# Shared transposes, one state load per batch and turned state reads in a fused attention kernel on one core

## The chip, the core and the metric

The program runs on one core of a Trainium2 chip: TensorE (PE; its weight loads are shown as PEld), VectorE (DVE), ScalarE (ACT), GpSimd (POOL) and SyncE (SP), which here issues every DMA. The metric is the time of one launch in device microseconds, the median of several runs.

## The reference

Inputs are x (8 batches, 8 heads, 512 positions, 64 wide), state (8, 8, 32, 64), a gate, and query, key and value weights for 4 experts, with an output weight for each. Per batch and head:

```
a     = softmax(x state^T / 8);   xread = a state      # x reads the state
a2    = softmax(state x^T / 8);   sread = a2 x         # the state reads x
X     = [xread; sread], heads side by side             # 544 rows of 512
w     = softmax over the best 2 of the 4 gate logits X w_gate
q,k,v = X wq[e], X wk[e], X wv[e]                       # 64 wide
y     = sum over e of w_e * causal_softmax(q k^T / 8) v wo[e]
```

## The kernel before

Most operands are kept as an fp16 high part and an fp16 remainder, so that a product is three matmuls (PROD). A batch has 512 rows, four tiles of 128 positions, and 32 state rows, which two batches share in a tail.

For each batch `front` (`first` for batch 0) splits x into parts and transposes them (xT<-xh), scores x against the state and back (`state_scores`), and makes gs, v, keys (kt) and queries. Queries leave PSUM through `masked` (qf), are split (qh) and are transposed by one DMA per tile into qm, line 813. `side` makes the reads of the state: line 844 ff. normalise the exponentials e2 with the reciprocal sum s2 while a2 and its remainder are written, two DMAs transpose a2 to a2t, and 48 matmuls with weights xh (128x128) and 64 moving columns of a2t give sr, already transposed, which `hi_lo` writes into xt_tail in two halves of 64 partitions (line 867).

The main part works on four blocks per batch, each two banks of scores (one per expert of the pair). `probs` (line 911) multiplies qm and kt, takes masked maxima (mx), writes exponentials (p32), splits them into ph and transposes each block by a DMA of its own into pt (line 957). `reads` (line 969) multiplies pt and v, scales by c6 into z32, splits into zh, transposes by a DMA for each block (line 996), multiplies z with wo_n and stores the block. Block k is read two steps after its scores. The last batch takes its blocks in falling order and transposes three of the four z on TensorE. `tail` does the same for the 64 state rows of two batches.

Nothing is issued where it is written: each step is recorded, and `Steps.run` issues the steps in the order of the table ORDER (step number, then which engine of an either/or, then fillers of zeros on TensorE); SLOTS says which buffer of a tag each use takes. Every engine runs its own instructions in that order. SP is one queue in order: an issue whose source is not ready holds all behind it. The recorded instructions all have line 364, so names of tiles tell them apart.

Of the kernel before, what the change touches and what calls it, by code (L numbers as in the profile page):

```python
# [19 lines left out]
           TSPAN=1.3, TOFF=1.2, KT=3, p32=3, ph=3, at=1, et=1, gs=1, xh=4, a2=2, o=4, sn=1, qf=2, qh=3, n_eb=1, n_e2=1,  # L20
           n_a2t=2, n_xt_tail=2, n_z32=3, n_z=3, n_zh=3, n_tq=1, n_tv=2, n_tpt=2, n_tz=2)
# [133 lines left out]
    "o": "0132322013203232131310203213023012",  # L155
    "tw2": "0100",
    "twg": "0101",
    "m4": "0111",
    "tmt": "0101",
    "tmx": "0101",  # L160
    "tpt": "0100",
# [1009 lines left out]
```

## Time and profile before

| | us |
|---|---|
| median of 3 runs (lowest, highest) | 305.74 (305.38, 306.52) |
| the profiled execution | 302.81 |
| its span on the core | 301.0 |
| PE, DVE, ACT, POOL busy | 279.7, 249.5, 215.6, 203.7 |

The span is what views of the trace cover; 1.8 us of the profiled execution lie around it. Busy time counts an engine's instructions, not SP's issues, which are read from the order of time of that queue.

### The profile page before, as it was taken

The page shows a single profiled execution, that of the slowest core. Times are in us where ns is not written, and L with a number is a line of the kernel's source. Part 1 is how long each engine was busy: PE and PEld are TensorE (multiplying, and loading weights), DVE is VectorE, ACT ScalarE, POOL GpSimd, SP SyncE. Part 2 cuts the span into 40 slices and gives each one's busy share as a digit, 9 for nine tenths or more (in the row PEclk, how much of TensorE's full clock was granted, in tenths as well). Part 3 has the DMA queues.
Part 4 walks back from the last instruction along what each step waited for, and adds up shares of the span by engine and source line. Part 5 has one row for each costly group of instructions (what it writes and reads, how often), then busy time and mean ns, then how long its engine had stood idle before and what let it go on. Part 6 is the DMA issues. An engine that isn't in the chain of part 4 may idle for free.

```text
span 301.0 us, 8936 instructions
## 1 busy us (share of the span) xinstructions
PE 279.7 (93%) x3194; PEld 187.5 (62%) x3196; DVE 249.5 (83%) x791; ACT 215.6 (72%) x687; POOL 203.7 (68%) x285
## 2 busy tenths in 40 slices
PE   8998897999899969798999997989899999999994
PEld 4876554667566635767556673865557667657862
DVE  1789999999899867998999998798779876888731
ACT  3497799698799776956899777666676667445652
POOL 7173785868787994867798675775776898446310
PEclk9999999999999989999999999999999999999999
DMA  7938669999999999999988999998893788889864
GB/s 193 200 129 147 167 143 193 222 174 169 218 182 194 191 165 211 188 195 227 215 129 167 176 185 239 174 201 180 150 159 73 139 171 158 194 134 163 170 203 175
DMA packets 155820, 53.16 MB, mean 177 GB/s; under 512 B 141824, under 2 KB 151296, under 8 KB 155776
## 3 DMA queue, kind: packets, MB, share of 16 engines
q1 hardware_dynamic: 155776, 52.59, 89.7%
q8 instruction: 25, 0.41, 0.6%
q14 instruction: 19, 0.16, 0.1%
HBM read 11.02 MB, written 8.91 MB: 66 GB/s over the span
## 4 chain that ended last, share of the span: by engine, by line
PE 42%; DVE 18%; DMA 12%; ACT 12%; POOL 9%; issue 6%; SPq 0%; POOLq 0%; DVEq 0%; ACTq 0%
PE bank L364 40%; DMA qm<-qh 7%; DMA pt<-ph 5%; DVE bank L364 4%; POOL ph L364 3%; ACT p L364 2%; POOL qh L364 2%; ACT xh L364 2%; DVE xh L364 2%; DVE v L364 2%; DVE qf L364 2%; PE bank L362 2%; DVE z L364 1%; DVE m L364 1%; POOL eb L364 1%
## 5 line engine op out<-in xcount | busy, mean ns | idle before, releaser
L364 PE MATMUL bank<-kt,qm 128*128 128x128 f16 (+13 forms) x368 | 51.3, 319 | 2.4 <-DMA qm<-qh 2.2
L364 PE MATMUL bank<-gs,at 128*128 128x260 f16 (+3 forms) x368 | 49.8, 283 | 1.5 <-DVE v L364 1.0
L364 POOL TENSOR_TENSOR ph<-p,ph 128x512 f16<-128x512 f32 (+3 forms) x29 | 41.7, 1438 | 10.3 <-ACT ph L364 6.8
L364 PE MATMUL bank<-wo_n,z 128*128 128x512 f16 (+1 forms) x198 | 46.1, 373 | 2.2 <-DVE c L364 1.1
L364 PE MATMUL bank<-v,pt 128*128 128x192 f16 x480 | 44.5, 246 | 1.6 <-DMA pt<-ph 0.9
L364 PEld LDWEIGHTS <-pt 128*128 128x128 f16 x480 | 39.8, 97 | 5.7 <-issue 2.2
L364 PEld LDWEIGHTS <-at 128*128 128x128 f16 x336 | 32.2, 98 | 8.9 <-issue 1.1
L364 ACT ACTIVATE p<-bank,mx 128x128 f32<-128x128 f32 (+3 forms) x64 | 33.2, 523 | 3.8 <-DVE mx L364 3.1
L364 DVE CUSTOM_DVE_ANT_0 bank<-bank,causal 128x128 f32<-128x128 f32 (+3 forms) x64 | 30.2, 501 | 6.6 <-PE bank L364 6.4
L364 PEld LDWEIGHTS <-qm 128*128 128x128 f16 (+1 forms) x336 | 20.6, 97 | 21.0 <-issue 8.4
L364 PEld LDWEIGHTS <-z 128*128 128x128 f16 x198 | 18.9, 98 | 20.5 <-DMA z<-zh 2.7
L364 ACT ACTIVATE o<-bank 128x512 f32<-128x512 f32 (+1 forms) x35 | 19.9, 584 | 8.3 <-PE bank L364 4.1
L364 PE MATMUL bank<-at,gs 128*128 128x512 f16 (+1 forms) x100 | 23.7, 379 | 0.5 <-DVE eb L364 0.5
L364 POOL TENSOR_TENSOR qh<-qf,qh 128x384 f16<-128x384 f32 x20 | 18.8, 946 | 2.6 <-ACT qh L364 2.2
L364 DVE TENSOR_TENSOR z<-bank,c 128x384 f32<-128x384 f32 x32 | 17.5, 548 | 3.1 <-PE bank L364 1.5
L364 POOL TENSOR_TENSOR zh<-z,zh 128x256 f16<-128x256 f32 x22 | 14.8, 676 | 6.4 <-ACT zh L364 2.9
L364 ACT ACTIVATE xh<-xn 128x512 f16<-128x512 f32 x32 | 18.9, 625 | 0.2 <-DMA xn<-in_x_dram 0.2
L364 DVE SCALAR_TENSOR_TENSOR qf<-bank,m 128x384 f32<-128x384 f32 x32 | 16.9, 546 | 2.0 <-PE bank L364 1.1
L364 POOL TENSOR_TENSOR z<-z 128x128 f32<-128x128 f32 x24 | 13.0, 544 | 7.6 <-DVE sums L364 4.1
L364 ACT ACTIVATE bank<-bank 128x4 f32<-128x4 f32 (+4 forms) x55 | 8.9, 164 | 12.6 <-DVE bank L364 5.8
L364 ACT ACTIVATE gs<-bank 128x512 f16<-128x512 f32 (+3 forms) x33 | 14.8, 471 | 2.4 <-PE bank L364 2.3
L364 POOL TENSOR_SCALAR ph<-p 128x1024 f16<-128x1024 f32 (+3 forms) x11 | 8.9, 812 | 10.6 <-ACT p L364 6.6
(206 smaller groups left out, 674.2 us busy)
## 6 DMA issues: line engine op xcount, KB each, us to landing
out_dram<-o SPq DMA_DIRECT2D x33, 256.0 KB, 2.7
xn<-in_x_dram SPq DMA_DIRECT2D x14, 512.0 KB, 4.6
xn<-in_x_dram SPq DMA_DIRECT2D x4, 256.0 KB, 3.4
sn<-in_state_dram SPq DMA_DIRECT2D x16, 32.0 KB, 4.0
p<-in_moe_wo_dram SPq DMA_DIRECT2D x2, 256.0 KB, 3.9
pt<-ph SPq DMA_TRANSPOSE x32, 3.9
z<-zh SPq DMA_TRANSPOSE x29, 2.6
xT<-xh SPq DMA_TRANSPOSE x28, 3.5
```

Of the source, the lines that this page charges most:

```text
L362: self.nc.tensor.matmul(out=to[:, :], lhsT=self.zeros[:, :128], rhs=self.zeros, start=True, stop=True, skip_group_check=True)
L364: f(**{k: v.ap() if isinstance(v, View) else v for k, v in kw.items()})
```

## The change

z of blocks 0 and 1, and of 2 and 3, goes into one zh and is transposed by one DMA (batches 0 to 6; both blocks' outputs follow it). Queries of two tiles share one qh and one DMA (batches 1 to 7). The probabilities of blocks 0 and 1 share one ph and one DMA (batches 0 to 6). A batch's state comes in one DMA. In the state reads a2 stays unnormalised; a2t (128x32) is the weight and xh moves 64 columns, in four column groups of the array, 96 matmuls; the result is scaled by s2 on DVE (rd), transposed on TensorE by one f32 transpose, and split by `hi_lo` on all partitions. The mask buffer of batch 0 shares the tail's tqf. ORDER and SLOTS are new tables.

```diff
-           ... qf=2, qh=3, n_eb=1, n_e2=1, n_a2t=2, n_xt_tail=2, n_z32=3, n_z=3, n_zh=3, ...
+           ... qf=2, qh=2, n_eb=1, n_e2=1, n_a2t=2, n_xt_tail=2, n_z32=3, n_z=2, n_zh=2, ...
...
     def load_state(b, after):
-        for c in range(2):
-            st.dma(sns[b // 2][:, b % 2, c], state[b].rearrange("(j c) n d -> c n j d", c=2)[c], 0.2, ...)
+        st.dma(sns[b // 2][:, b % 2], state[b].rearrange("(j c) n d -> n j c d", c=2), 0.35, after=after)
...
-            qh = st.buf("qh", [P, 2, 6 * D], F16, bufs=CFG["qh"])
-            split(6 * D, qh[:, 0], qh[:, 1], qf)
-            st.dma(qm[:, t]..., qh.rearrange("p a n -> p (a n)"), 0.675, transpose=True)
+            if t % 2 == 0:
+                qh = st.buf("qh", [P, 2, 2, 6 * D], F16, bufs=CFG["qh"])
+            split(6 * D, qh[:, t % 2, 0], qh[:, t % 2, 1], qf)
+            if t % 2:
+                st.dma(qm[:, t - 1:t + 1]..., qh.rearrange("p t a n -> p (t a n)"), 1.35, transpose=True)
...
-            f = s2[:, g:g + 1]
-            st.either([("POOL", ... out=a2[:, 0], in0=e2[:, g], scalar1=f ...), ("ACT", ... scale=f)])
-            low(512, a2[:, 1], e2[:, g], f, a2[:, 0])
+            split(512, a2[:, 0], a2[:, 1], e2[:, g])
...
+        n = [(t, a, c) for t in range(T) for a, c in PROD]
+        st.mm([(sr[HJ[j], g * D:(g + 1) * D], a2t[:, g, c, t, HJ[j]], xh[t // 2][:, t % 2, a, (2 * j + g) * D:(2 * j + g + 1) * D], i == 0, i == len(n) - 1)
+               for g in range(2) for i, (t, a, c) in enumerate(n) for j in range(H // 2)], (96, 64, 128, 4))
+        rd = st.buf("rd", [P, 2, D], F32, bufs=1)
+        dve(2 * D, nc.vector.tensor_tensor, out=rd, in0=sr[:, :2 * D]..., in1=s2.unsqueeze(2).broadcast_to([P, 2, D]), op=ALU.mult)
+        tr = bank("tr")
+        st.transposes([(tr[:, :P], rd.rearrange("p c d -> p (c d)"))], ident, 0.11)
+        hi_lo(P, xt[:, 0, :, c0, :], xt[:, 1, :, c0, :], tr[:, :P].rearrange("p (j n) -> p j n", n=NS), 2.0)
...
-        st.dma(pt.rearrange("p a c q -> p (a c) q"), ph[:, :2 * n], 0.000875 * 2 * n, transpose=True)
+        if not joint:
+            st.dma(pt, ph[:, :2 * n], 0.000875 * 2 * n, transpose=True)
+        elif i == 1:
+            st.dma(phs[b, "pt"], ph[:, :1536], 0.000875 * 1536, transpose=True)
...
-            split(E * D, zh[:, 0], zh[:, 1], z32)
-            st.dma(z.rearrange("p a r q -> p (a r) q"), zh.rearrange("p a c -> p (a c)"), 0.45, transpose=True)
+            split(E * D, zh[:, i % 2, 0], zh[:, i % 2, 1], z32)
+            if b == B - 1:
+                st.dma(z2[:, i % 2]..., zh[:, i % 2]..., 0.45, transpose=True)
+            elif i % 2:
+                st.dma(z2.rearrange("p i a r q -> p (i a r) q"), zh.rearrange("p i a c -> p (i a c)"), 0.9, transpose=True)
+            if b < B - 1 and i % 2 == 0:
+                return
+        for i in (i - 1, i) if b < B - 1 else (i,):
+            outs(b, i, z2)
```

On the SP queue, the stretch that carries the queries of batch 3 (qm<-qh) reads before as follows; z is the output side of an earlier batch, xT the x of a later one, sn the state, and 128x6x128 means six squares of 128.

```order
L364 DMA_TRANSPOSE qm_103<-qh_184 128x6x128
L364 DMA_TRANSPOSE z_168<-zh_171 128x4x128
L364 DMA_TRANSPOSE qm_103<-qh_183 128x6x128
L364 DMA out_dram<-o_176 128x512
L364 DMA_TRANSPOSE xT_101<-xh_92 128x8x128
L364 DMA_TRANSPOSE xT_101<-xh_93 128x8x128
L364 DMA out_dram<-o_174 128x512
L364 DMA sn_87<-in_state_dram 128x1x64
L364 DMA_TRANSPOSE qm_103<-qh_182 128x6x128
L364 DMA_TRANSPOSE z_169<-zh_173 128x4x128
L364 DMA_TRANSPOSE z_168<-zh_172 128x4x128
L364 DMA_TRANSPOSE qm_103<-qh_184 128x6x128
```

The same stretch of SP in the changed kernel:

```order
L362 DMA_TRANSPOSE qm_103<-qh_181 128x12x128
L362 DMA out_dram<-o_174 128x512
L362 DMA_TRANSPOSE z_169<-zh_171 128x8x128
L362 DMA_TRANSPOSE xT_101<-xh_93 128x8x128
L362 DMA_TRANSPOSE xT_101<-xh_91 128x8x128
L362 DMA out_dram<-o_176 128x512
L362 DMA out_dram<-o_175 128x512
L362 DMA_TRANSPOSE qm_103<-qh_180 128x12x128
```

Four issues of six squares became two of twelve, and three of z became one of eight: from the first queries to the last, 12 issues became 8.

On PE, the end of the state reads of batch 3 before (bank takes sr, pt are probabilities):

```order
L364 MATMUL bank_85<-a2t_146,xh_92 128x64
L364 LDWEIGHTS xh_92
L364 MATMUL bank_85<-a2t_146,xh_92 128x64
L364 LDWEIGHTS pt_0_154
L364 MATMUL bank_86<-v_0_115,pt_0_154 128x192
```

And on PE in the changed kernel, the end of the same reads (gs and at belong to the values of the next batch):

```order
L362 MATMUL bank_82<-xh_93,a2t_146 32x64
L362 LDWEIGHTS a2t_146
L362 MATMUL bank_82<-xh_93,a2t_146 32x64
L362 LDWEIGHTS gs_100
L362 MATMUL bank_80<-at_99,gs_100 128x512
```

Weight and moving operand have changed places, and each product writes 32 partitions. On PE further on, the transpose of the scaled result (rd) of that batch in the changed kernel:

```order
L362 LDWEIGHTS at_99
L362 MATMUL bank_86<-gs_100,at_99 128x260
L362 MATMUL bank_79<-ident,rd_151 128x128
L362 LDWEIGHTS pt_0_155
L362 MATMUL bank_80<-v_0_115,pt_0_155 128x192
```

This transpose is new, and 36 matmuls of other work stand between the last state read and it.

## Rows read from the trace of the kernel before

**Rows 1.** by stretch: stretch, length, busy (instructions) PE PEld DVE ACT POOL, clock, DMA share, GB/s

```profile
25.00:50.00 25.00, 21.38 (x198) 12.31 (x199) 24.16 (x85) 21.26 (x73) 16.94 (x24) 1.00 0.76 164
50.00:225.00 175.00, 162.42 (x1971) 108.35 (x1969) 155.96 (x495) 135.94 (x447) 130.99 (x155) 0.99 1.01 187
225.00:297.00 72.00, 71.92 (x798) 49.71 (x795) 53.11 (x183) 41.95 (x132) 42.36 (x52) 1.00 0.77 158
100.00:125.00 25.00, 22.25 (x260) 12.99 (x258) 19.45 (x49) 19.64 (x60) 19.88 (x21) 0.93 1.07 188
```

**Rows 2.** the page, shares of the chain that ended last, by engine

```profile
PE 42%; DVE 18%; DMA 12%; ACT 12%; POOL 9%; issue 6%; SPq 0%; POOLq 0%; DVEq 0%; ACTq 0%
```

**Rows 3.** the chain in order of time (start, length, what)

```profile
70.43 5.79 DMA qm<-qh
...
105.99 5.53 DMA qm<-qh
...
237.62 2.81 DMA qm<-qh
...
241.26 56.00 PE bank L364 x580
```

**Rows 4.** order of time on SP, 146 to 151 us (start, length)

```profile
146.18 0.58 SPq L364 DMA_DIRECT2D out_dram<-o  x1
146.80 0.56 SPq L364 DMA_DIRECT2D sn<-in_state_dram  x1
147.46 1.26 SPq L364 DMA_TRANSPOSE qm<-qh  x1
148.83 2.50 SPq L364 DMA_TRANSPOSE z<-zh  x2
```

**Rows 5.** per tile: issues on SP, ns min/median/max, first and last start

```profile
L364 SPq DMA_TRANSPOSE z<-zh x29: 1189/1218/2367, 59.2 to 285.5; - x29
...
L364 SPq DMA_TRANSPOSE qm<-qh x28: 1210/1244/2478, 66.7 to 269.3; - x28
...
L364 SPq DMA_TRANSPOSE xT<-xh x28: 1233/1296/2734, 21.2 to 204.8; - x28
...
L364 SPq DMA_TRANSPOSE pt<-ph x32: 1199/1413/3432, 42.4 to 283.8; - x32
...
L364 SPq DMA_DIRECT2D sn<-in_state_dram x16: 541/591/2469, 2.3 to 179.9; - x16
```

**Rows 6.** DMA issues: count, median us from issue to landing

```profile
pt<-ph SPq DMA_TRANSPOSE x32, 3.9
...
qm<-qh SPq DMA_TRANSPOSE x28, 3.2
```

**Rows 7.** order of time on PE, two places (start, length)

```profile
88.09 1.56 PE L364 MATMUL bank<-a2t,xh 128*128 128x64 f16 x48 [0.52 <-DMA a2t<-a]
89.48 0.75 PE L364 MATMUL bank<-v,pt 128*128 128x192 f16 x7
...
100.38 1.18 PE L364 MATMUL bank<-wn,bd 64*32 64x260 f16 x48
101.48 0.33 PE L364 MATMUL bank<-ident,sn 128*128 128x128 f32 x1
101.65 2.75 PE L364 MATMUL bank<-wo_n,z 128*128 128x512 f16 x12
...
110.38 0.99 PE L364 MATMUL bank<-xT,bd 64*32 64x512 f16 x24 [2.37 <-ACT p L364]
```

**Rows 8.** groups by form: count, busy us, mean ns, idle before

```profile
L364 POOL TENSOR_TENSOR qh<-qf,qh 128x384 f16<-128x384 f32 x20 | 18.8, 946 | 2.6 <-ACT qh L364 2.2 <-DVE mx L364 0.3
...
L364 DVE SCALAR_TENSOR_TENSOR qf<-bank,m 128x384 f32<-128x384 f32 x32 | 16.9, 546 | 2.0 <-PE bank L364 1.1
...
L364 DVE SCALAR_TENSOR_TENSOR a<-e,s,a 128x512 f16<-128x512 f32 x9 | 10.1, 1130 | 0.0
...
L364 ACT ACTIVATE qh<-qf 128x384 f16<-128x384 f32 x19 | 9.9, 523 | 2.2 <-DVE qf L364 1.9 <-DMA qm<-qh 0.2
```

More of the change, by code (lines that the diff above doesn't have):

```diff
@@ L19 @@
            LEAN={'DVE': 1.0, 'ACT': 0.3, 'POOL': 0.3}, W0=-33, PACE=37.0, LAG=2, FRONT=1.5, FSPAN=1.0,
-           TSPAN=1.3, TOFF=1.2, KT=3, p32=3, ph=3, at=1, et=1, gs=1, xh=4, a2=2, o=4, sn=1, qf=2, qh=3, n_eb=1, n_e2=1,
-           n_a2t=2, n_xt_tail=2, n_z32=3, n_z=3, n_zh=3, n_tq=1, n_tv=2, n_tpt=2, n_tz=2)
+           TSPAN=1.3, TOFF=1.2, KT=3, p32=3, ph=3, at=1, et=1, gs=1, xh=4, a2=2, o=4, sn=1, qf=2, qh=2, n_eb=1, n_e2=1,
+           n_a2t=2, n_xt_tail=2, n_z32=3, n_z=2, n_zh=2, n_tq=1, n_tv=2, n_tpt=2, n_tz=2)
 XT = 1.85
@@ L29 @@
 ORDER = """
[92 rows of a table removed]
[90 rows of a table added]
 """
 SLOTS = {
-    "bank": ("102346573102467653276267450267453721520347637102165341020346120356710657132457040257560237560215367057465342506217345625"
-          "301652743014675321407563254013624710347651027361275641273412505062731473057462031547604512460257412736161426031726035417"
-          "624105342651036216630512715425743126750341652701653642745631074532174054137205736314657431463057"),
-    "xh": "0123013210230123",
-    "p32": "02101022210122010210211021201201021012012",
-    "mb": "11010101",
-    "sbm": "10110010",
-    "m2": "01110101",
-    "kt": "020102012",
-    "s2": "00001010",
-    "lg": "1101010011011",
-    "gs1": "0100010110101",
-    "gt1": "0100100010010",
-    "bd": "0101010",
-    "gs2": "0101100100101",
-    "gw": "1011011001100",
-    "m6": "01100111",
-    "qf": "01101010101010100101101010011011",
-    "wgt": "10110101",
-    "a2": "0101100110101010",
-    "qm": "01110100",
-    "mx": "01230010201312031032113021032120",
-    "a2t": "01010110",
-    "sums": "01010101",
-    "ph": "01201021012012201201201201202102",
-    "xt_tail": "0011",
-    "c6": "0010101010010101",
-    "z32": "00120201022102120120210210201212",
-    "zh": "01201120102102210121120121021",
-    "z": "01201201201010210212012012120121",
-    "qh": "1021012021020120120120120210",
-    "o": "0132322013203232131310203213023012",
-    "tw2": "0100",
@@ new lines @@
+    "bank": ("032154267031452613153615264030231705321463753260413425310615720435606726314253170235106275210675460217125071562136107346"
+          "147206513742031563470214501376054321605423706352106752107564217352601024357610423715061240573165027316743132626270617423"
+          "07146750275134727651236540712451324160231675034572603175620643260415614356174356105617232403245104726103"),
+    "xh": "0231021302312013",
+    "p32": "01202102020102021021020102102120120201201",
+    "mb": "11000100",
@@ new lines @@
+    "sbm": "10110100",
+    "m2": "01000010",
+    "bd": "0101010",
+    "kt": "012021020",
+    "s2": "01010101",
+    "lg": "0100110101011",
+    "gs1": "0010000101100",
+    "gt1": "0111010100101",
+    "a2": "0101010110101001",
+    "gs2": "0101001101010",
+    "gw": "0100100101001",
+    "m6": "10000101",
+    "qf": "10101010101010010101100101011001",
+    "a2t": "01110010",
+    "qm": "01110010",
+    "wgt": "01010101",
+    "mx": "21311032210321010330201320211301",
+    "sums": "01101001",
@@ L157 @@
+    "ph": "1021201200120120201201201",
+    "xt_tail": "0010",
+    "c6": "0010101001010100",
+    "z32": "02101201201020202101210210201012",
+    "zh": "001110110100101",
+    "qh": "01101010101010",
+    "z": "001010110010101001",
+    "o": "2013122012301323010133202203121302",
+    "tw2": "0001",
+    "m4": "0001",
+    "tmt": "1101",
     "twg": "0101",
-    "m4": "0111",
-    "tmt": "0101",
     "tmx": "0101",
-    "tpt": "0100",
-    "tc4": "0100",
-    "tz": "00",
+    "tpt": "0111",
+    "tc4": "1011",
@@ L164 @@
+    "tz": "10",
 }
@@ L581, in state_read_then_moe_attention @@
     xns, sns, marks = {}, {}, {}
-    m6s, khs = {}, {}
+    phs = {}
+    m6s, khs, zs, zhs = {}, {}, {}, {}
     consts, sums, c6s = {}, {}, {}
@@ L611, in load_state @@
     def load_state(b, after):
-        for c in range(2):
-            st.dma(sns[b // 2][:, b % 2, c], state[b].rearrange("(j c) n d -> c n j d", c=2)[c], 0.2, after=after, par=(0.2, 8, 0.55))
+        st.dma(sns[b // 2][:, b % 2], state[b].rearrange("(j c) n d -> n j c d", c=2), 0.35, after=after)
     def parts_of_x(xh, xn, t):
@@ L666, in first @@
         xn, sn = xns.pop(b), sns[b // 2]
-        bd = st.buf("bd32", [P, H // 2, 2, NS])
+        bd = st.buf("tqf", [P, 2, P], F32, seen=((("rearrange", ("p k q -> p (k q)",), {}), ("rearrange", ("p (j c n) -> p j c n",), dict(j=H // 2, c=2))), [P, H // 2, 2, NS]))
         st.do("POOL", 0.3, (lambda out: nc.gpsimd.memset(out, 0.0)), out=bd)
@@ L810, in front @@
             qf = masked(b, t, qp)
-            qh = st.buf("qh", [P, 2, 6 * D], F16, bufs=CFG["qh"])
-            split(6 * D, qh[:, 0], qh[:, 1], qf)
-            st.dma(qm[:, t].rearrange("p a k q -> p (a k) q"), qh.rearrange("p a n -> p (a n)"), 0.675, transpose=True)
+            if t % 2 == 0:
+                qh = st.buf("qh", [P, 2, 2, 6 * D], F16, bufs=CFG["qh"])
+            split(6 * D, qh[:, t % 2, 0], qh[:, t % 2, 1], qf)
+            if t % 2:
+                st.dma(qm[:, t - 1:t + 1].rearrange("p t a k q -> p (t a k) q"), qh.rearrange("p t a n -> p (t a n)"), 1.35, transpose=True)
         base = st.base
@@ L836, in state_scores @@
             dve(512, nc.vector.tensor_reduce, out=m2[:, g:g + 1], in_=sa, axis=AX.X, op=ALU.max, negate=True)
-            small(1, m2[:, g:g + 1], m2[:, g:g + 1], 0.0, f, False)
+            small(1, m2[:, g:g + 1], m2[:, g:g + 1], 14 * math.log(2.0) / f, f, False)
             act(512, e2[:, g], sa, AF.Exp, bias=m2[:, g:g + 1], scale=f, accum_out=s2[:, g:g + 1])
@@ L843, in side @@
         for g in range(2):
-            small(1, s2[:, g:g + 1], s2[:, g:g + 1], EPS, 2.0 ** -14, False)
+            small(1, s2[:, g:g + 1], s2[:, g:g + 1], EPS * 2.0 ** 14, 1.0, False)
         dve(2, nc.vector.reciprocal, out=s2, in_=s2)
@@ L849, in side @@
             a2 = st.buf("a2", [P, 2, S], F16, bufs=CFG["a2"])
-            f = s2[:, g:g + 1]
-            st.either([("POOL", 0.673, (nc.gpsimd.tensor_scalar, dict(out=a2[:, 0], in0=e2[:, g], scalar1=f, scalar2=1.0, op0=ALU.mult, op1=ALU.mult))),
-                       ("ACT", 0.613, (nc.scalar.activation, dict(out=a2[:, 0], in_=e2[:, g], func=AF.Copy, scale=f)))])
-            low(512, a2[:, 1], e2[:, g], f, a2[:, 0])
+            split(512, a2[:, 0], a2[:, 1], e2[:, g])
             st.dma(a2t[:, g].rearrange("p a t q -> p (a t) q"), a2.rearrange("p a s -> p (a s)"), 0.9, transpose=True)
@@ L859, in side @@
         sr = bank("sr")
-        for j0 in range(0, H // 2, CFG["SM"]):
-            g = []
-            for j in range(j0, j0 + CFG["SM"]):
-                o = sr[:, j * 64:(j + 1) * 64].rearrange("p (c n) -> p c n", c=2)
-                g += chain((o, xh[t // 2][:, t % 2, a, j * P:(j + 1) * P], a2t[:, :, c, t, HJ[j]])
-                           for t in range(T) for a, c in PROD)
-            st.mm(g, (len(g), 64, 128, 1), into=[xt[:, :, :, c0]])
-        for c in range(2):
-            h = slice(c * D, (c + 1) * D)
-            hi_lo(P, xt[h, 0, :, c0, :], xt[h, 1, :, c0, :],
-                  sr[h, :H // 2 * 64].rearrange("p (j c n) -> p j c n", c=2, n=NS)[:, :, c, :], 2.0 ** -13)
+        n = [(t, a, c) for t in range(T) for a, c in PROD]
+        st.mm([(sr[HJ[j], g * D:(g + 1) * D], a2t[:, g, c, t, HJ[j]], xh[t // 2][:, t % 2, a, (2 * j + g) * D:(2 * j + g + 1) * D], i == 0, i == len(n) - 1)
+               for g in range(2) for i, (t, a, c) in enumerate(n) for j in range(H // 2)], (96, 64, 128, 4))
+        rd = st.buf("rd", [P, 2, D], F32, bufs=1)
+        dve(2 * D, nc.vector.tensor_tensor, out=rd, in0=sr[:, :2 * D].rearrange("p (c d) -> p c d", c=2), in1=s2.unsqueeze(2).broadcast_to([P, 2, D]), op=ALU.mult)
+        tr = bank("tr")
+        st.transposes([(tr[:, :P], rd.rearrange("p c d -> p (c d)"))], ident, 0.11)
+        hi_lo(P, xt[:, 0, :, c0, :], xt[:, 1, :, c0, :], tr[:, :P].rearrange("p (j n) -> p j n", n=NS), 2.0)
     def gate(gb, n, scale):
@@ L913, in probs @@
         w = P * (i + 1)
-        ph = st.buf("ph", [P, 4 * S], F16, bufs=CFG["ph"])
-        pt = st.buf(f"pt{i}", [P, 2, 2 * (i + 1), P], F16, bufs=1)
-        pts[b, i] = pt
+        joint = i < 2 and b < B - 1
+        if not joint or i == 0:
+            phs[b] = st.buf("ph", [P, 4 * S], F16, bufs=CFG["ph"])
+        if i >= 2:
+            pt = st.buf(f"pt{i}", [P, 4 * (i + 1), P], F16, bufs=1)
+        else:
+            if (b, "pt") not in phs:
+                phs[b, "pt"] = st.buf("pt01", [P, 12, P], F16, bufs=1)
+            pt = phs[b, "pt"][:, 8 * i - 4 * i:4 + 8 * i]
+        h0 = 512 * (joint and i == 1)
+        ph = phs[b]
+        pts[b, i] = pt.rearrange("p (a c) q -> p a c q", a=2)
         sp = [bank(f"sp{s}") for s in range(2)]
@@ L955, in probs @@
         n = 2 * w
-        split(n, ph[:, :n], ph[:, n:2 * n], p32[:, :n])
-        st.dma(pt.rearrange("p a c q -> p (a c) q"), ph[:, :2 * n], 0.000875 * 2 * n, transpose=True)
+        split(n, ph[:, h0:h0 + n], ph[:, h0 + n:h0 + 2 * n], p32[:, :n])
+        if not joint:
+            st.dma(pt, ph[:, :2 * n], 0.000875 * 2 * n, transpose=True)
+        elif i == 1:
+            st.dma(phs[b, "pt"], ph[:, :1536], 0.000875 * 1536, transpose=True)
         if (i % 2 == 1) == (b < B - 1):
@@ L986, in reads, with outs @@
         z32 = z32[:, 2 * D:]
-        z = st.buf("z", [P, 2, 2, P], F16, bufs=CFG["n_z"])
+        if i % 2 == 0 or b == B - 1:
+            zs[b] = st.buf("z", [P, 2, 2, 2, P], F16, bufs=CFG["n_z"])
+        z2 = zs[b]
         if b == B - 1 and i < CFG["ZL"]:
             zt = bank("zt")
-            st.transposes([(zt[:, r * P:(r + 1) * P], z32[:, r * P:(r + 1) * P]) for r in range(2)], ident, 0.22, into=[z])
-            hi_lo(2 * P, z[:, 0], z[:, 1], zt[:, :2 * P].rearrange("p (r q) -> p r q", r=2), 1.0)
-        else:
-            zh = st.buf("zh", [P, 2, E * D], F16, bufs=CFG["n_zh"])
-            split(E * D, zh[:, 0], zh[:, 1], z32)
-            st.dma(z.rearrange("p a r q -> p (a r) q"), zh.rearrange("p a c -> p (a c)"), 0.45, transpose=True)
+            st.transposes([(zt[:, r * P:(r + 1) * P], z32[:, r * P:(r + 1) * P]) for r in range(2)], ident, 0.22)
+            hi_lo(2 * P, z2[:, i % 2, 0], z2[:, i % 2, 1], zt[:, :2 * P].rearrange("p (r q) -> p r q", r=2), 1.0)
+        else:
+            if i % 2 == 0 or b == B - 1:
+                zhs[b] = st.buf("zh", [P, 2, 2, E * D], F16, bufs=CFG["n_zh"])
+            zh = zhs[b]
+            split(E * D, zh[:, i % 2, 0], zh[:, i % 2, 1], z32)
+            if b == B - 1:
+                st.dma(z2[:, i % 2].rearrange("p a r q -> p (a r) q"), zh[:, i % 2].rearrange("p a c -> p (a c)"), 0.45, transpose=True)
+            elif i % 2:
[4 more added lines that the diff above has]
+            outs(b, i, z2)
+    def outs(b, i, z2):
         o = st.buf("o", [P, DM], F32, bufs=CFG["o"])
@@ L1001, in reads @@
                 op = bank("op")
-                st.mm(chain((op[:, :DM // 2], z[:, a, pr, :], wo_n[:, c, pr, w]) for pr in range(2) for a, c in PROD), (6, DM // 2, 128, 1), into=[o[:, w]])
+                st.mm(chain((op[:, :DM // 2], z2[:, i % 2, a, pr, :], wo_n[:, c, pr, w]) for pr in range(2) for a, c in PROD), (6, DM // 2, 128, 1), into=[o[:, w]])
                 act(DM // 2, o[:, w], op[:, :DM // 2], scale=2.0 ** -18)
@@ L1006, in reads @@
         op = bank("op")
-        st.mm(chain((op, z[:, a, pr, :], wo_n[:, c, pr, :]) for pr in range(2) for a, c in PROD), (6, 512, 128, 1), into=[o])
+        st.mm(chain((op, z2[:, i % 2, a, pr, :], wo_n[:, c, pr, :]) for pr in range(2) for a, c in PROD), (6, 512, 128, 1), into=[o])
         act(DM, o, op, scale=2.0 ** -18)
```

182 rows, old and new, of the table ORDER are left out of this document.

## The prediction

> **What bounds the kernel now.** I read the view by stretch first, then the chain, then the order of time on the queue that the change shortens. From 225 to 297 us TensorE is busy for 71.92 of 72.00 us; from 50 to 225 for 162.42 of 175, and from 25 to 50 for 21.38 of 25 [rows 1]. So the last quarter is bound by TensorE's own work, which the chain confirms: from 241.26 us on it is 56 us of matmuls [rows 3]. Ahead of it TensorE is idle for 12.58 + 3.62 = 16.2 us. In 100 to 125 us the granted clock is 0.93, so about 3.5 us passed at 1.2 instead of 2.4 GHz, behind a wait of 2.37 us at 110.38 [rows 1, 7]; half of these, 1.75 us, is lost. What scheduling can give back is 18.0 us at most, and the rest only comes from less work on TensorE.
>
> Who holds TensorE up ahead of 225 us? In the chain PE has 42%, DVE 18%, DMA 12%, ACT 12%, POOL 9% [rows 2]; the DMA pieces are above all transposes of queries, 5.79 us at 70.43 and 5.53 at 105.99 [rows 3]. Their queue hardly rests: from 146.18 to 151.33 us SP issues an output, a state load and three transposes, 4.90 us of issuing in 5.15 [rows 4]. An issue of a transpose costs SP 1.22 us at four squares (z), 1.24 at six (qm), 1.30 at eight (xT) and 1.41 at the mix of four to sixteen (pt), by medians [rows 5]. It hardly grows with size, so joining transposes is worth something on this queue. DVE is the other engine near its limit: 24.16 of 25 us from 25 to 50 [rows 1].
>
> **The change part by part.** The sum is made against the profiled execution, 302.81 us (span 301.0 and 1.8 around it); the median of the runs, 305.74, is 1.0097 times that, and each saving is scaled by this at the end.
>
> *Issues on SP.* z: 28 issues of 1.218 us (34.1) become 14 of eight squares, priced like xT at 1.296 (18.1): 16.0 less. Queries: 28 of 1.244 (34.8) become 14 of twelve squares; the nearest row is pt, 1.413 (19.8): 15.0 less. Probabilities: 14 of 1.413 become 7 of the same: 9.9 less. State: 8 issues of 0.591 less, 4.7. Together 45.6 us of issuing [rows 5]. If an issue grew in proportion to its squares, only the 4.7 of the state loads would be left; the row of xT, with twice the squares of z at 1.06 times the price, is much nearer to the first value, which I take. None of it is time on the chain by itself. The DMA share of the idle is what it can reach: 12 of the 58 points that the chain spends off TensorE, 21% of 18.0, is 3.7 us, which I take. The bounds are 0 (every freed issue is followed by a wait for its source) and half of all the idle, 9.0 us (later steps of other engines start earlier too).
>
> In the Trainium skill, "DMA: Bandwidth & Descriptors", section "Issuing engines are not separate DMA queues", the sequencer's time to start a DMA is called usually small relative to the DMA itself. By that the joined transposes, which move the same bytes, give nothing, and the sum loses its 3.7 us; the rows here disagree, since SP is taken for 4.90 of 5.15 us by issuing. That no run here shows a joined transpose keeps it among the rivals.
>
> *State reads on TensorE.* 48 matmuls take from 88.09 to the next at 89.48, 1.39 us, or 29 ns each, eight times in the program. After, 96 matmuls write 32 partitions each, in four column groups. If four run side by side at 29 ns, it is 24 x 29 = 0.70 us. Changing the form of the array costs something: the 48 matmuls of eight groups at 100.38 take 1.10 us up to the next, where six rounds of 260 columns at the rate of the row at 101.65 (2.75 us for 12 of 512 columns, so about 0.115 us) are 0.69, an excess of 0.41; I take half of it, 0.20, since that stretch holds two products. The transpose of rd is like that of sn at 101.48, 0.17 us to the next. So 0.70 + 0.20 + 0.17 = 1.07 in place of 1.39: 0.32 x 8 = 2.6 us less [rows 7]. Bounds: without excess 4.2 less; if column groups don't run side by side, 96 x 29 ns = 2.78, and with the rest 3.15, 14.1 us more. I take 2.6, because in the row with eight groups the groups plainly do overlap. The transpose of rd has 36 matmuls in front of it in batch 3, enough to hide the scaling on DVE; without that cover PE would stand for about one DVE instruction (0.55 us by qf [rows 8]) per batch.
>
> *a2 and its remainder.* On DVE nine remainders of 1.130 us go [rows 8]; the order has two subtractions and one copy there instead, none dearer than that, and eight scalings rd, each below the 0.546 us of qf with a third of its columns. So at least 6 x 1.13 - 8 x 0.55 = 2.4 us less on DVE, and the separate scaling of e2 on POOL goes with it. DVE and POOL hold 27 of the 58 points, 8.4 us of the idle; I take 2 of these, between 0 and 4.
>
> *Waits that the change adds.* The first of two tiles now waits for the second: six matmuls (0.69), masking on DVE (0.546), the high part on ACT (0.523), the remainder on POOL (0.946), 2.7 us [rows 7, 8], and lands with a transpose of the size of pt, 3.9 instead of 3.2 us [rows 6]: 3.4 us later. Behind the joint issue on SP stand z, x and outputs. What hides it: before, the fourth issue of a batch stood eleven rows behind the first, now the second stands seven behind it, so the last tile is earlier by about four issues, some 5 us, and the first tile's lead over its scores must carry 3.4. z of an even block waits for the odd one, but only an output product hangs on it. The probabilities of block 0 wait for block 1, one block of a lag of two. I cost these at nothing while the queue is shorter, and the rival below prices them. The new order moves everything else too; I have no row for that but the idle it may use or add, up to 4 us either way.
>
> Sum: -3.7 - 2.6 - 2.0 = -8.3; 294.5 for the profiled execution, and 305.74 - 8.4 = 297.3 us.
>
> **The rivals.**
> 1. *The queue's relief is hidden.* SP then waits for its sources instead of issuing, and the DMA engines, whose mean share is 1.01 from 50 to 225 us [rows 1], move the same bytes. For it: that share. Against it: in the stretch shown SP goes from issue to issue. Only the 2.6 of TensorE are left: 305.74 - 2.6 = 303.1 us, or up to 305 if the order costs 2.
> 2. *Joint queries come too late.* The first scores of a batch wait for a transpose that waits for its second tile. For it: the chain already ends on qm at 70.43, 105.99 and 237.62 [rows 3]. At three such places 3.4 us each is 10.2, against 8.3 saved: 1.9 more, 307.7 us, slower. It decides from three places on (8.3 / 3.4 = 2.4). Against it: the queue ahead of those issues is shorter by some 5 us.
> 3. *Column groups of 32 don't run side by side.* Each of the 96 matmuls takes its 29 ns, 14.1 us more in place of 2.6 less: 305.74 + 14.1 - 5.7 = 314.1 us. The point from which it decides is a stretch of state reads of 2.1 us. Against it is the row with eight groups.
>
> On the third, the Trainium skill, "TensorEngine Tiling (Array Packing)", section "Restrictions and Gotchas", says that column tiling is mutually exclusive with Fast Weight Load. It would make weights the price, as rival 3 has it; the trace of the 64x32 form, 48 matmuls in 1.10 us, doesn't show such a price.
>
> **How the numbers follow.** The forecast, 297.3 us, has a chance of 0.62, rival 1 0.20, rival 2 0.13, rival 3 0.05. The forecast's own range is 292 (4.2 of TensorE and 9 of idle) to 302 (4 lost to the order). The range given, 292 to 307, takes in rival 1 and the near half of rival 2. About 0.5% (1.5 us) is what a measurement of this kernel can tell from no change. Faster by more: 0.61 of the forecast, 0.14 of rival 1, together 0.75. Within it: 0.01, 0.06 and 0.04, together 0.11. Slower: 0.09 of rival 2 and 0.05 of rival 3, 0.14.
>
> **What would show it.** State reads of about 0.9 us up to the next matmul, 2.1 or more for rival 3. Issues of z and qm on SP of 1.3 and 1.4 us at the median, 14 each, and gaps between issues ahead of 225 us. TensorE busy for a larger share from 25 to 225 us, with its idle down from 16.2 to about 10, and the DMA's share of the chain below 12%. Rival 2 would show as matmuls kt,qm that wait for the DMA of qm longer than before. The prediction is wrong if the issue of a joint transpose costs 2 us or more, or if the idle of TensorE doesn't fall.

## The result and the profile after

| | before | after |
|---|---|---|
| median of the runs, us (lowest, highest) | 305.56 (303.04, 306.52) | 293.38 (290.58, 297.09) |
| ratio to before, 95% interval | | 0.958 (0.948, 0.968) |
| profiled execution, span, us | 302.81, 301.0 | 294.01, 292.2 |
| PE busy, idle in the span, us | 279.7, 21.3 | 274.2, 18.0 |
| DVE, ACT, POOL busy, us | 249.5, 215.6, 203.7 | 246.0, 212.5, 198.2 |

The changed kernel is 12.2 us faster by the medians and 8.8 by the two profiled executions: TensorE is busy for 5.5 us less and idle for 3.3 less. A second timing gave 294.07 us, ratio 0.954 (0.943, 0.965). Ratios are of means that leave out executions more than 1.5% above the fastest of their kernel, while the medians take in all.

By stretch (length; busy of PE, PEld, DVE, ACT, POOL with instructions; granted clock; DMA share; GB/s), to read against [rows 1]:

```profile
25.00:50.00 25.00, 21.61 (x260) 13.90 (x259) 24.20 (x85) 22.04 (x77) 19.35 (x25) 1.00 0.90 177
50.00:225.00 175.00, 167.10 (x2407) 112.36 (x2404) 163.29 (x526) 139.35 (x460) 140.47 (x161) 0.99 1.05 192
225.00:288.00 63.00, 62.59 (x714) 42.75 (x699) 44.79 (x150) 35.58 (x117) 28.12 (x34) 1.00 0.83 166
50.00:75.00 25.00, 23.76 (x388) 16.76 (x386) 24.34 (x74) 20.66 (x68) 20.23 (x24) 0.93 1.02 182
```

From 25 to 225 us TensorE is now idle for 3.39 + 7.90 = 11.3 us, 16.2 before. One stretch still has the granted clock at 0.93 of the higher level, some 3.5 us at 1.2 GHz, now from 50 to 75 us.

The chain of the changed kernel, by engine, and its DMA pieces with the last run of matmuls (start, length, what):

```profile
PE 59%; DVE 26%; DMA 7%; issue 4%; ACT 2%; POOL 2%; DVEq 0%; ACTq 0%
```

```profile
104.19 5.54 DMA qm<-qh
...
165.82 8.92 DMA pt<-ph
...
224.63 4.92 DMA pt<-ph
229.60 57.62 PE bank L362 x653
```

PE has 59% where it had 42, the DMA 7 where it had 12 [rows 2]. These shares are rough: in another execution of the changed kernel PE has 49% and the DMA 10. The chain of before holds five pieces of queries, three of them in [rows 3], and three of probabilities; one of queries and two of probabilities are left.

SP's queue at the like place of [rows 4] (start, length), then its issues by tile as in [rows 5] (ns, minimum/median/maximum), then medians to landing as in [rows 6]:

```profile
146.42 0.57 SPq L362 DMA_DIRECT2D out_dram<-o  x1
147.04 1.30 SPq L362 DMA_TRANSPOSE z<-zh  x1
148.44 1.75 SPq L362 DMA_TRANSPOSE pt<-ph  x1
150.28 1.71 SPq L362 DMA_TRANSPOSE xT<-xh  x1
152.09 1.49 SPq L362 DMA_TRANSPOSE qm<-qh  x1
```

```profile
L362 SPq DMA_TRANSPOSE z<-zh x15: 1191/1289/2023, 63.3 to 275.3; - x15
...
L362 SPq DMA_TRANSPOSE qm<-qh x14: 1322/1488/2500, 69.0 to 258.1; - x14
...
L362 SPq DMA_TRANSPOSE pt<-ph x25: 1189/2072/4834, 43.5 to 272.6; - x25
...
L362 SPq DMA_DIRECT2D sn<-in_state_dram x8: 612/640/1613, 1.8 to 108.8; - x8
```

```profile
pt<-ph SPq DMA_TRANSPOSE x25, 4.8
...
z<-zh SPq DMA_TRANSPOSE x15, 3.9
qm<-qh SPq DMA_TRANSPOSE x14, 3.9
```

Joint z and queries cost SP what was forecast, about a single issue each. Summed over all rows of the queue, SP issues for 213.6 us instead of 250.1: z 38.3 to 20.5, queries 39.1 to 23.5, state 13.7 to 6.7, probabilities 53.5 to 54.0.

The medians of probabilities, 1.41 and 2.07 us, belong to different mixes of sizes. Before has eight issues each of four, eight, twelve and sixteen squares; of the 25 after, 15 have twelve squares (seven joint, eight single) and eight sixteen. Sorted by size, in the order in which the program issues them, those of before took 1.25, 1.27, 1.45 and 2.46 us at the median. So the price does grow, steeply from twelve to sixteen squares. One batch of before, four to sixteen squares (start, length):

```profile
80.33 1.22 SPq L364 DMA_TRANSPOSE pt<-ph  x1
...
84.39 1.30 SPq L364 DMA_TRANSPOSE pt<-ph  x1
...
88.21 1.45 SPq L364 DMA_TRANSPOSE pt<-ph  x1
...
92.63 1.74 SPq L364 DMA_TRANSPOSE pt<-ph  x1
```

The seven joint issues took 12.4 us (1.33 to 2.61 each) where the fourteen that they replace took 19.1. The other eighteen, the same in both kernels, took 41.6 where they had taken 34.4; why they became dearer isn't shown.

The state reads in the order of time on PE, to set beside 88.09 and 89.48 of [rows 7], and groups that answer to [rows 8]:

```profile
84.56 0.96 PE L362 MATMUL bank<-xh,a2t 128*32 128x64 f16 x96
85.45 0.30 PE L362 MATMUL bank<-identh,m 128*64 128x128 f16 x4
...
166.04 0.27 PE L362 MATMUL bank<-ident,rd 128*128 128x128 f32 x1
166.15 1.66 PE L362 MATMUL bank<-v,pt 128*128 128x192 f16 x18
```

```profile
L362 DVE TENSOR_TENSOR rd<-bank,s 128x128 f32<-128x128 f32 x8 | 2.2, 277 | 0.1
...
L362 DVE TENSOR_TENSOR a<-e,a 128x512 f16<-128x512 f32 x2 | 1.4, 682 | 0.0
...
L362 POOL TENSOR_TENSOR a<-e,a 128x512 f16<-128x512 f32 x14 | 16.8, 1197 | 1.5 <-POOL mtail L362 0.9 <-ACT a L362 0.5
```

96 matmuls take 0.89 us to the next here, 48 took 1.39; the transpose of rd adds 0.11. In the six batches of each kernel in which no wait falls inside, 96 take 0.89 to 1.05 us and 48 took 1.40 to 1.50.

### The profile page after: what moved, and what is told of

It is laid out like the page before. It is cut to its first block, busy times and chain, and to the rows that moved or that the text cites. A ratio compares the mean times of both kernels' runs of the same rounds, so it can differ in the third digit from the quotient of the medians.

```text
span 292.2 us, 9588 instructions
## 1 busy us (share of the span) xinstructions
PE 274.2 (94%) x3587; PEld 184.1 (63%) x3587; DVE 246.0 (84%) x787; ACT 212.5 (73%) x685; POOL 198.2 (68%) x268
## 3 DMA queue, kind: packets, MB, share of 16 engines
q1 hardware_dynamic: 154528, 52.59, 94.6%
## 4 chain that ended last, share of the span: by engine, by line
PE 59%; DVE 26%; DMA 7%; issue 4%; ACT 2%; POOL 2%; DVEq 0%; ACTq 0%
PE bank L362 57%; DMA pt<-ph 5%; DVE xh L362 4%; DVE bank L362 3%; DVE gs L362 2%; DVE qf L362 2%; DVE sbm L362 2%; DMA qm<-qh 2%; DVE eb L362 2%; PE bank L360 2%; DVE m L362 2%; DVE mb L362 1%; DVE z L362 1%; DVE et L362 1%; POOL qh L362 1%
## 5 line engine op out<-in xcount | busy, mean ns | idle before, releaser
L362 PE MATMUL bank<-gs,at 128*128 128x260 f16 (+3 forms) x368 | 51.4, 285 | 1.8 <-ACT e L362 1.0
L362 PE MATMUL bank<-kt,qm 128*128 128x128 f16 (+13 forms) x368 | 48.0, 313 | 2.2 <-DMA qm<-qh 1.1
L362 PEld LDWEIGHTS <-pt 128*128 128x128 f16 x480 | 40.5, 98 | 9.6 <-DMA pt<-ph 6.6
L362 POOL TENSOR_TENSOR ph<-p,ph 128x1024 f16<-128x1024 f32 (+3 forms) x25 | 36.0, 1443 | 7.3 <-ACT ph L362 2.9
L362 PEld LDWEIGHTS <-at 128*128 128x128 f16 x336 | 32.7, 99 | 11.3 <-issue 3.3
L362 PE MATMUL bank<-at,gs 128*128 128x512 f16 (+1 forms) x100 | 24.7, 382 | 0.7 <-ACT at L362 0.7
L362 DVE SCALAR_TENSOR_TENSOR xh<-xn,xh 128x512 f16<-128x512 f32 x23 | 19.2, 854 | 5.2 <-ACT xh L362 5.2
L362 POOL TENSOR_SCALAR ph<-p 128x1024 f16<-128x1024 f32 (+3 forms) x12 | 11.1, 929 | 17.3 <-ACT p L362 11.8
L362 POOL TENSOR_TENSOR zh<-z,zh 128x256 f16<-128x256 f32 x25 | 18.1, 728 | 4.6 <-ACT zh L362 3.3
L362 POOL TENSOR_TENSOR qh<-qf,qh 128x384 f16<-128x384 f32 x18 | 16.3, 913 | 3.9 <-ACT qh L362 1.5
L362 POOL TENSOR_TENSOR a<-e,a 128x512 f16<-128x512 f32 x14 | 16.8, 1197 | 1.5 <-POOL mtail L362 0.9
```

The source lines that it names most:

```text
L362: f(**{k: v.ap() if isinstance(v, View) else v for k, v in kw.items()})
```

## The experiments

The question was whether the gain belongs to the parts (fewer issues, shorter state reads) or to the order that was laid out with them. First, from the side of the changed kernel, each part was undone. Before's own median lies between 305.56 and 307.85 us over the sets of runs, so kernels are compared by their ratio to before, timed beside each.

**The changed kernel again, and its three joint transposes issued as two each, back to back in their place** (35 issues more, same buffers, same order):

```diff
-  st.dma(phs[b, "pt"], ph[:, :1536], ..., transpose=True)
+  st.dmas([(phs[b, "pt"][:, 0:4], ph[:, 0:512]), (phs[b, "pt"][:, 4:12], ph[:, 512:1536])], ...)
...                                      # likewise z by block, queries by tile
```

> The changed kernel once more, as the reference of this set. Every theory expects 0.96 of the kernel before (0.948 to 0.968 so far), some 293 us.

> The changed kernel in its own order, with each joint transpose (z, queries, first probabilities) issued as two DMAs back to back in its place: 35 more issues on SP, the same squares moved, the same waits. If it is the number of issues that the change saved (first theory), SP is busy some 30 to 45 us longer, the idle of TensorE ahead of its last stretch grows, and the time rises by 4 to 8 us, to 297 to 301 us. If the bytes are what counts and the gain came from the new order or the state reads (rival), it stays within 1.5 us of the changed kernel.

308.48 us, ratio 1.010 (1.006, 1.014): 14.4 us more by the medians, 16 to 17 by the ratios, far above both expectations. SP issues for 253.2 us again. The DMA engines' own time hardly differs (94.6% of 292.2 us, 276, and 90.2% of 308.9 us, 279), so it isn't the bytes that cost. A relief of issues that I had put at 3.7 us is worth the whole gain, in this order. But both issues stand where the joint one stood, so the first half still waits for the second: the run prices 35 issues at these places and not a kernel laid out without joining.

**The old state reads in the new order** (in this kernel a buffer of state rows is overwritten early, which changes some values and no work):

```diff
-  96 matmuls sr[HJ[j], ...] = a2t x xh; rd = sr * s2; one transpose of rd; hi_lo on 128 partitions
+  a2 and its remainder scaled by s2; 48 matmuls sr = xh x a2t; hi_lo in two halves of 64
```

> The changed kernel in its own order, with the state reads of the kernel before: a2 normalised while it is written, 48 matmuls with 128 weight columns, no scaled copy and no transpose on TensorE, two halves written. If the turned reads gave TensorE work back (first theory: 1.39 us against about 1.1 per batch, and less on DVE and POOL), the time rises by 2 to 5 us, to 295 to 298 us, with PE's work up by some 2.5 us. If they lie off the path (rival), it stays within 1.5 us of the changed kernel.

305.47 us, ratio 0.997 (0.993, 1.001): 11.4 more, 12 to 13 by the ratios, again the whole gain. The two costs sum to 26 us where there were 12 to lose, so neither can be read as that part's share.

**Half the bytes in the old kernel.** Queries and z are transposed by their high parts alone (the remainders are left out of the products):

```diff
-  st.dma(qm[:, t]..., qh..., transpose=True)
+  st.dma(qm[:, t, 0], qh[:, 0], transpose=True)     # and z, zh likewise
```

> The kernel before, in its own order, with the transposes of queries and of z moving only the high parts (142 of 996 squares less, the same number of issues); products use the high part in place of the remainder, so the remainders are left out of the result. If SP's issues bound the queue (first theory), an issue still takes about 1.2 us and the time stays within 1.5 us of the kernel before, 304 to 307 us. If the bytes bound it (rival), it falls by 4 us or more, to 302 us or less.

305.54 us, ratio 0.997 (0.993, 1.002), though the DMA share from 50 to 225 us (last column but one, beside [rows 1]) fell from 1.01 to 0.89:

```profile
50.00:225.00 175.00, 162.59 (x1971) 108.46 (x1968) 157.52 (x498) 136.97 (x449) 132.95 (x155) 0.99 0.89 169
```

A seventh of the squares less gains nothing in the old order. What an order laid out for fewer bytes would gain, the run can't tell.

**The parts in the old order.** Then from the other side: each part, and both, in the order table of before, where a step was moved only if a dependency asked for it (a joint issue stands where the later of the two stood; with joint issues z, zh and qh have two buffers of double size, as in the changed kernel, where before had three).

```diff
-  order of before, parts of before
+  order of before, state reads turned                 # reads
+  order of before, joint z, qm, pt; one state load    # joint
+  order of before, all of these                       # both
```

> The order of before, with one part of the change alone: the state reads turned (96 short matmuls a batch with the state rows as the moving side, the reciprocal and the turning back). Theory one, each part acts by itself in any order: the reads are some 0.3 to 0.4 us shorter a batch on TensorE and a2 cheaper on VectorE and GpSimd, 8 batches, so 302 to 303 us against 306. Rival, the gain comes from the new order being fitted to the parts: an order laid out for the old durations leaves it within 2 us of before (304 to 308).

> The order of before, with the joint transposes of z, queries and first probabilities and the one state load per batch alone (each joint issue stands where the later of the two stood). Theory one, SP's issuing binds wherever it stands: SP spends some 35 us less on issues and the time falls by 7 to 9 us, to 297 to 299. Rival, the fit of the order: steps stay where the old landings put them, and the first halves now come later, so within 2 us of before or slower (304 to 312).

> Both parts in the order of before, steps moved only where a dependency asks for it. Theory one, the parts add: 294 to 296 us, the whole gain without the new order. Rival, the fit: 302 to 308, and the rest of the gain belongs to the new order.

All three are slower than before: 312.02 us, ratio 1.011 (1.003, 1.019); 320.24, 1.041 (1.035, 1.046); 322.88, 1.048 (1.041, 1.055). The two with joint issues are slower than either theory gave; for the reads alone the interval still takes in the rival's 2 us, and TensorE is idle for 30.2 us there, 21.3 before, by no one wait that stands out. In the last, TensorE isn't busier by much (282.6 us) but idle for 38.4 of a span of 321.0. SP issues for only 211.0 us in the kernel with joint issues, 39 less than before, and the time rises by 12. What TensorE waited for (us in total, times, longest) shows much of why; first before, then that kernel:

```profile
PE bank L364 <- DMA qm<-qh: 2.2, 4, 1.0
```

```profile
PE bank L404 <- DMA qm<-qh: 7.7, 5, 2.8
PE bank L404 <- DMA z<-zh: 5.9, 4, 2.1
```

That is 13.6 us of waits instead of 2.2 (z is not among before's), 11.4 of the 14.4 us by which TensorE's idle time grows between the two profiles (21.3 to 35.7). By the forms of the matmuls that wait, four of the five waits for queries, 4.95 us, end at block 0 or 2, the first tile of its pair. The longest, 2.75 us, ends at block 3 of the last batch, which is taken first there, so it isn't a first tile waiting for a second. The output products of the first z were moved to right behind the joint issue, with no work laid in between, so part of their 5.9 us is made by the mending. For the queries it is my second rival, and the mechanism is real. In the changed kernel the same waits are small:

```profile
PE bank L362 <- DMA qm<-qh: 1.1, 1, 1.1
...
PE bank L362 <- DMA z<-zh: 0.6, 1, 0.6
```

The kernel with both parts also has four slices with a lower granted clock, where before and the changed kernel have one stretch each in the profiles read here, and another execution of the changed kernel has two (tenths of the higher level, in 40 slices):

```profile
PEclk9999997999997999999999979999979999999999
```

**Only the matmuls of the state reads undone in the new order,** a2 left as in the changed kernel:

```diff
-  96 matmuls sr[HJ[j], ...] = a2t x xh; rd = sr * s2; one transpose of rd; hi_lo on 128 partitions
+  48 matmuls sr = xh x a2t; hi_lo in two halves of 64, by a constant in place of s2
```

> The changed kernel with the 48 long state matmuls a batch and their evacuation in two halves as before, with a2 taken as the changed kernel takes it; the normalisation of the state part by its sum is left out (a constant scale stands in its place). It parts the 11.4 us that the old reads as a whole cost in the new order. Theory one, TensorE's own time: 0.3 to 0.4 us a batch on a TensorE that has almost no idle time, 296 to 297 us. Rival one, the fit: any longer step in this order costs some 10 us, 302 to 306. If it stays under 297, the rest of the 11.4 us lies in the normalised a2 on VectorE and GpSimd.

299.91 us, ratio 0.976 (0.970, 0.982): about two points above the changed kernel's 0.954 and 0.958, some 6 us, between the two expectations. If the two add, about half of the 11.4 is TensorE's reads and evacuation and the rest the normalised a2: in the kernel with all of the old reads POOL is busy for 209.6 us and DVE for 251.4, here for 197.0 and 245.5. Its span is 5.7 us longer, 4.5 of it busy time of PE (278.7) and 1.2 idle.

**Each joint transpose undone alone, and the new order without either part:**

```diff
-  st.dma(qm[:, t - 1:t + 1]..., qh..., transpose=True)
+  st.dmas([(qm[:, t - 1 + u]..., qh[:, u]...) for u in range(2)], ...)
...                                      # or z alone, or pt alone, or all three with the old state reads
```

> The changed kernel, with only the joint transposes of queries issued as two, back to back in their place: 14 issues more on SP (all three kinds split, 35 more, cost 14.4 us). If the cost goes by the number of issues, 14.4 x 14/35 = 5.8 us more, 299 to 301 us. If it goes by which data is late, the queries, which the first scores of each two tiles wait for, carry most of it: 8 us or more, 302 and above.

> The changed kernel, with only the joint transposes of z issued as two in their place: 14 issues more. By number of issues 5.8 us more, 299 to 301 us. If it goes by which data is late, little, since only an output product hangs on z: under 2 us more, below 296.

> The changed kernel, with only the joint transposes of the first two blocks' probabilities issued as two in their place: 7 issues more. By number of issues 2.9 us more, 296 to 298 us. A rival is that the joint one, which lands in 4.8 us against 3.9 before and holds TensorE up for 3.0 us at 171.6 us, is too long a piece for its place: then splitting it costs nothing or gains up to 2 us, 291 to 294.

> The new order with neither part: the three joint transposes issued as two each and the old state reads (state loads stay joint; as in the run with the old reads, a part of the state rows is overwritten early, which changes values and no work). If each part's undoing spoils the order by itself, the two costs overlap and the time is 305 to 311, near the worse of the two. If they add, 293.5 + 14.4 + 11.4 = 319 us. Were the order by itself the gain, it would be under 300, which the runs so far speak against.

| split in two | us | ratio (95%) | span, PE busy, PE idle |
|---|---|---|---|
| nothing (changed kernel) | 293.38 | 0.958 (0.948, 0.968) | 292.2, 274.2, 18.0 |
| queries | 302.38 | 0.989 (0.977, 1.001) | 301.2, 279.2, 22.0 |
| z | 299.71 | 0.981 (0.971, 0.991) | 299.5, 276.1, 23.4 |
| probabilities | 293.73 | 0.962 (0.950, 0.973) | 294.1, 275.4, 18.7 |
| all three | 308.48 | 1.010 (1.006, 1.014) | 308.9, 278.7, 30.2 |
| all three, old reads | 316.63 | 1.037 (1.027, 1.047) | 314.8, 283.0, 31.8 |

Queries cost 9 us, z 6, probabilities nothing that can be measured. That queries cost more than z isn't clear of the noise, as the two intervals show. The count of issues gave 5.8 us for z and meets it, but it gave 2.9 us between z or queries and probabilities, where 6.0 and 8.7 were measured. "Little hangs on z" was wrong. Splitting the probabilities brings their issuing from 54.0 to 59.1 us, so joining them does save SP 5 us in this order, and the time doesn't follow. That the long joint piece is itself what holds TensorE up at 171.6 us was wrong too: with it split, the gap there is 2.9 us as before. What TensorE waits for there is the single transpose of block 3, of sixteen squares, whose issue alone held SP for 4.83 us in the changed kernel (SP, then PE):

```profile
165.82 4.83 SPq L362 DMA_TRANSPOSE pt<-ph  x1
```

```profile
174.78 2.17 PE L362 MATMUL bank<-v,pt 128*128 128x192 f16 x24 [2.95 <-DMA pt<-ph]
```

In the kernel with split queries the place where half the loss arises can be read in the order of time on PE (start, length, form, idle before):

```profile
86.45 0.30 PE L366 MATMUL bank<-identh,m 128*64 128x128 f16 x4
88.96 2.74 PE L366 MATMUL bank<-wo_n,z 128*128 128x512 f16 x6 [2.21 <-DMA z<-zh]
...
91.71 3.08 PE L366 MATMUL bank<-v,pt 128*128 128x192 f16 x18
```

```profile
86.00:96.00 10.00, 7.79 (x83) 4.90 (x84) 6.10 (x20) 6.62 (x22) 4.47 (x8) 0.66 1.18 198
```

z, which SP issues at 83.91 us where the changed kernel has it at 81.41, holds TensorE up for 2.2 us, and behind that wait the granted clock of these 10 us is 0.66 (last column but two): some 6.8 us at 1.2 GHz, in which 3.4 are lost. The same 18 matmuls of probabilities take 3.08 us here and 1.66 at the higher level. So this wait of 2.2 us costs about 2.2 + 3.4. It need not be so: behind the wait of 2.95 us at 174.78 the changed kernel keeps a granted clock of 1.00 from 174 to 180 us, and in another execution of the same kernel, behind 2.84 us at the same place, it is 0.72.

With neither part the new order takes 316.6 us: slower than before, and a little below the sum of the two undoings (293.4 + 14.4 + 11.4 = 319). All eight in one table, as ratios to before:

| | order of before | new order |
|---|---|---|
| neither part | 1 | 1.037 (state loads joint) |
| state reads alone | 1.011 | 1.010 (state loads joint) |
| joint issues alone | 1.041 | 0.997 |
| both | 1.048 | 0.958 |

In the old order each part costs time, in the new order each takes off 3 to 5%, and the order alone loses. Only the parts with the order laid out for them win. In the new order's rows without joint issues the first half still waits for the second.

## Why the prediction was right, and where its steps were not

The forecast of 297.3 us was 3.9 too high, inside its range. The sum for the profiled execution, -8.3, met -8.8, in part by luck: 2.6 of it was to be work of TensorE and 5.7 idle time, and measured are 5.5 of work and 3.3 of idle time. By groups, the state reads went from 12.7 us to 8.2 and 2.2 for the new transpose; the matmuls kt,qm, the same 368, went from 51.3 to 48.0, which I had nowhere and no run explains. The rest of the 3.9 is that before's median lies 0.9% above its profiled execution and the changed kernel's 0.2% below, so scaling by 1.0097 carried over an offset that the changed kernel doesn't have.

*Issues on SP.* Of the 45.6 us, 36.5 came. z (17.8 for 16.0), queries (15.6 for 15.0) and state loads (7.0 for 4.7) came as priced by the nearest rows; the term of the probabilities, 9.9, was mis-sized: their issuing rose by 0.5. I had priced them by a median over four sizes; the joint ones saved 6.7 and the single ones of twelve and sixteen squares became dearer by 7.2. That an issue hardly grows with size held up to twelve squares and not at sixteen (2.46 us). The gaps between issues came: from 25 to 225 us SP issues for 158.5 us, 179.1 before. The step that fails is the one behind it, that 21% of the idle, 3.7 us, is what the relief is worth. There is no such worth apart from the order: the same issues saved cost 12 us in the old order, and taken back in the new one they cost 14.4. Rival 1 (the relief is hidden behind the bytes) falls by that split, which moves the same bytes; halving them in the old order agrees.

The sentence of the Trainium skill that I weighed there ("DMA: Bandwidth & Descriptors", section "Issuing engines are not separate DMA queues": the time to start a DMA is usually small relative to the DMA itself) does not describe this queue: an issue of queries takes 1.24 of the 3.2 us to its landing [rows 5, 6], with the DMA share down by 0.12 nothing changed, and 14 issues more of the same bytes cost 9 us for queries and 6 for z.

*State reads.* 0.89 to 1.05 + 0.11 to 0.17 us where I had 1.07, against 1.39: the forecast 2.6 us over eight batches holds for TensorE's own stretch. Column groups of 32 do run side by side (rival 3 falls): 96 serial matmuls of 29 ns would take 2.78 us. The cover of 36 matmuls for the scaling was that of batch 3; six of the eight batches have 5 to 12, and TensorE still waited for rd only 0.4 us. In the new order the reads are worth about 6 us, by the run with the old matmuls; why more than 2.6 isn't shown.

*a2 and its remainder.* On DVE this part fell from 10.1 us to 4.0 with the scaling rd, more than the 2.4 that I had. On POOL it didn't fall: the new order makes 14 remainders there instead of 7, so the scaling that goes is outweighed, 14.8 us of a2 before and 20.0 after. In before these were (group, count, busy us, mean ns)

```profile
L364 POOL TENSOR_TENSOR a<-e,a 128x512 f16<-128x512 f32 x7 | 8.1, 1160 | 0.6
...
L364 POOL TENSOR_SCALAR e<-e,s 128x512 f32<-128x512 f32 x7 | 5.3, 757 | 2.8 <-ACT a L364 1.9 <-DMA pt<-ph 0.9
...
L364 POOL TENSOR_SCALAR a<-e,s 128x512 f16<-128x512 f32 x2 | 1.4, 696 | 0.1
```

That DVE as a whole is busy for 3.5 us less and POOL for 5.5 less comes from other choices of the new order too. Undone with the reads, a2 costs about 5 us more than the reads alone, against the 2.0 that I took.

*Added waits.* Queries landed in 3.9 us as forecast. I costed their later first tile at nothing "while the queue is shorter". What hides it is not the shorter queue, since that kernel in the old order has the shorter queue and loses 12 us. I put it down to the second tile's earlier place in the order, the other half of my reason (the last tile stands earlier); the rival that I gave 0.13 is what happens without it. That is in part argued: in batches 1 to 6 the issue with the second tile starts 3.3 us on average ahead of the first tile's scores before, 5.7 in the changed kernel, and in the old order with joint issues 5.3, its waits included.

*Idle of TensorE* was to fall from 16.2 to about 10 and fell to 11.3; the DMA's share of the chain was to fall below 12% and is 7, or 10 in another execution. What stays open is whether the old order could have been re-laid by hand for one part alone with a gain; the runs only show that mending its dependencies isn't enough. Nor was it tried to cover the wait ahead of 50 us that keeps the one slow stretch.

## What to carry to other kernels

Where the instructions of all queues stand in one fixed order, a part's worth isn't the time that it saves but what the re-laid order makes of it: judge part and order together. Neither way of taking them apart gives shares: undone from the finished kernel the parts cost 26 us where 12 were gained, and added to the old order they lose. Joining two transfers makes the first wait for the second, so draw forward what makes the second, or the saved issues turn into waits. A wait of some 2 us on TensorE can cost more than itself, if the clock falls behind it.

## What the runs showed of the hardware

- The price of a transpose issue on SP grows little up to twelve squares: 1.22 us at four and 1.24 at six (before), 1.29 at eight and 1.49 at twelve (z and queries of the changed kernel). At sixteen (probabilities of block 3) it is 2.46 us at the median before, from 1.32 to 3.43, and 2.83 in the changed kernel, up to 4.83.
- 96 matmuls with 32-column weights and 64 moving columns, in four column groups, follow one another every 9 to 11 ns (0.89 to 1.05 us for 96). Four side by side at the 29 ns of before's would be 0.70 us; whether the 0.19 to 0.35 left is the change of form isn't shown.
- The kernel with both parts in the old order has four stretches at 1.2 GHz where the main kernels have one each, or two in another execution of the changed kernel; with split queries one of them is 6.8 us long, behind a wait of 2.2 us for z, with 18 matmuls at 3.08 us instead of 1.66.
